# Weight gradients of a backward pass moved into the staging slots of the K and V gradients

## Chip, core and metric

The kernel runs on one core of a Trainium2 chip. The metric is the device time of one execution in microseconds, as the median of several runs; besides, one execution is recorded by the hardware profiler, and all views below are of that execution.

## The reference, cut to what matters

Two layers, each an attention over a long cache followed by a small dense block, are applied twice to one token with the same weights; the kernel computes the output and the gradients of the loss for the input, both caches and all weights.

```python
x = x + attention(layernorm(x), k_cache, v_cache, wq, wo)   # L1
x = x + mlp(layernorm(x), w1, b1, w2, b2)                   # L2: h = relu(n w1 + b1)^2; h w2 + b2
x = x + attention(layernorm(x), k_cache, v_cache, wq, wo)   # L3, same weights
x = x + mlp(layernorm(x), w1, b1, w2, b2)                   # L4, same weights
out, vjp = jax.vjp(f, x, k_cache, v_cache, wq, wo, w1, b1, w2, b2)
return out, *vjp(grad_out)
```

Sizes: D = 1024, 32 query heads in G = 4 groups of R = 8, head width 128, 65536 cached positions, F = 3584, all in bfloat16. Each cache has 67 MB, and so has its gradient. There is one token, so every weight gradient is an outer product, and as each weight is used in two layers, it is the sum of two outer products: a contraction over two rows. The four weight gradients together have 31.5 MB: `out_4` for wq (1024 x 4096), `out_5` for wo (4096 x 1024), `out_6` for w1 (1024 x 3584), `out_8` for w2 (3584 x 1024).

## The kernel before

The caches are streamed four times: forward for L1, forward for L3, a backward pass for L3 (`attn_bwd3`) and a last pass (`attn_bwd4`) that reads K and V once more and makes the gradients of both caches for both layers. The change is in this last pass and in what leads up to it.

SBUF is cut into 14 areas of 1 MB (128 partitions x 4096 bf16 elements). Two neighbours make a pair of 2 MB, so `pair[6]` is `area[6]` and `area[7]`. The exponentials of the two forward passes lie in `e_tiles`, one 1 MB tile a group and layer, and become free group by group in the last pass. A `Ring` hands out areas for reads in the order of their last use; `ring.once` adds areas that are used for one read and then leave it. A `Turn` hands out its areas in a circle. A read is issued by SP as soon as its area is free, in the order of the program; so the number of free areas sets how far reads run ahead.

The last pass goes over 256 items, 64 to a group, of 8 blocks of 128 positions. `pipeline` interleaves three steps: `vT` transposes the item's V, `vS` two items later makes the products with the output gradient and, every fourth item, the coefficients X (VectorE and, for the copies at L1033 and L1034, GpSimd) and their transposes, and `k8`, 7 items after `vT`, makes the query gradient and the cache gradients: matmuls at L1071 into `ps_gg`, evacuated by `evac` (L152 on ScalarE, L155 on VectorE, whichever has less planned load) into a staging slot. `ST` is a turn of three slots, `pair[6]`, `pair[8]` and `pair[10]`. Every four items fill one slot with 1 MB of K's and 1 MB of V's gradient, which GpSimd's queue (POOL) writes by two DMAs (L1078, L1079). Further tasks are hung on item numbers by `at(bg, i, fn)` and are put behind what is then queued on each engine (`in_order`).

The weight gradients are such tasks. `rows_into` first brings two vectors that lie across the partitions into two rows: it takes four columns at a time, with two casts (L1092), four matmuls with the identity (L1095) and one evacuation of 2 x 512. `outer2` then makes units of 128 x 1024, two matmuls (L1122) and an evacuation each, and writes every stage of 128 x 2048 (512 KB) by a DMA of POOL (L1126). The stages are five half-areas: four in the tiles `e_tiles` of the first group, free when that group is done, and one in `area[5]`. So the tasks run from item 73 on and are spread evenly up to item 244; the last group's part of wq follows the last item.

```python
ring.once(area[6], area[8], area[9], area[10], area[11])
for st, b in ((1, 0), (1, 1), (0, 0), (1, 2), (0, 1)):
    streams[st].fetch(ORD4[0], b)
...
at(bg, done[0], rows_ready)
i0, i1 = done[0] + 1, IPG * G - 12
tasks = list(gw_tasks())
for t, fn in enumerate(tasks):
    at(bg, i0 + t * (i1 - i0) // len(tasks), fn)
```

Before the first item, the first five halves of K and V are read ahead into the once-areas, and the ring's five areas are filled further; `og1.first` and `g_setup` prepare the first group. The rows of wo for the second group (`og1.later`) come as 256 KB DMAs into `first_rows` on SP's queue, up to 30 items ahead; the other rows of wo and wq go through `wo_rows`, three areas of 256 KB, on ScalarE's queue.

Of the kernel before, what the change touches and what calls it, by code (L numbers as in the profile page):

```python
# [8 lines left out]
BF = mybir.dt.bfloat16  # L9
# [5 lines left out]
P = 128  # L15
# [3 lines left out]
def kernel(  # L19
# [39 lines left out]
    GD = R * DH  # L59
# [8 lines left out]
    IPG = C // 8  # L68
    TLEAD = 2
    LAGV = TLEAD + IPG + 12  # L70
    SLOT = 4096
    OG = 2048
    SMALL = 8192

    def spool(name, bufs=1):
# [4 lines left out]
    tmp = spool("tmp", bufs=2)  # L80
# [8 lines left out]
    def ps_tr():  # L89
        return PS["pool"].tile([P, 8, P], BF, name="ps_tr", tag="tr", bufs=2 if PS["pass4"] else 3)  # L90
# [4 lines left out]
    def ps_gg():  # L95
        return PS["pool"].tile([P, 1024], F32, name="ps_gg", tag="gg", bufs=2)
# [26 lines left out]
    ident_b = const.tile([P, P], BF, name="ident_b")  # L123
# [18 lines left out]
    def evac(out, in_, kind="bf"):  # L142
        n = 1
        for d in in_.shape[1:]:
            n *= d
        if kind == "bf":
            ca, cd = 0.19 + n * 0.00081, 0.15 + n * 0.00053
        else:
            ca, cd = 0.19 + n * 0.00081, 0.15 + n * 0.00105
        if load["act"] + ca <= load["dve"] + cd:  # L150
            load["act"] += ca
            nc.scalar.copy(out=out, in_=in_)  # L152
# [10 lines left out]

    main = spool("main")
    ECP = R * CP
    e3_all = main.tile([P, G * ECP], BF, name="eT3")
    e_tiles = {1: [main.tile([P, ECP], BF, name="eT1_%d" % g)[:, :] for g in range(G)],
               3: [e3_all[:, g * ECP:(g + 1) * ECP] for g in range(G)]}
    area, pair, wides = [], {}, []
    for i in range(0, 14, 2):  # L170
        t = main.tile([P, 2 * SLOT], BF, name="pair%d" % i)
# [11 lines left out]
    def part(ap, i, n):  # L183
        return ap[:, i * n:(i + 1) * n]
# [70 lines left out]
    ring = Ring()  # L255
# [331 lines left out]
    def at(bg, i, fn):  # L587
        bg.setdefault(i, []).append(fn)
# [371 lines left out]
    def attn_bwd4(La, Lb, oga, ogb, order, eTa, eTb, dqT, bg, group_done, streams):  # L960
        lname = "B1"
        kit = items_of(order)
        n = len(kit)
# [5 lines left out]
        ST = Turn([pair[6], pair[8], pair[10]])  # L969
        DOB = vec.tile([P, G, 4, R2], BF, name="DOB")  # L970
        nc.vector.memset(DOB[:], 0.0)
        state = {}
# [127 lines left out]
    def outer2(stages, out_dram, a_rows, K, b_rows, c0, N):  # L1100

        KB = K // P
        ov = out_dram.rearrange("(p k) n -> p k n", k=KB)
        av = a_rows[:, 0:K].rearrange("q (p k) -> q k p", k=KB)
        st = {}
        pieces = []
        if 2 * N <= OG:
            per = OG // N
            pieces = [(kb, per, 0, N) for kb in range(0, KB, per)]
        else:  # L1110
            pieces = [(kb, 1, n0, min(OG, N - n0)) for kb in range(KB) for n0 in range(0, N, OG)]
        for kb, per, n0, w in pieces:
            for kk in range(per):
                for m0 in range(0, w, 1024):
                    def unit(kb=kb, per=per, n0=n0, w=w, kk=kk, m0=m0):
                        if kk == 0 and m0 == 0:
                            st["og"] = stages.next()
                        nn = min(1024, w - m0)
                        pg = ps_gg()
                        for q0 in range(0, nn, 512):  # L1120
                            qq = min(512, nn - q0)
                            nc.tensor.matmul(pg[:, q0:q0 + qq], lhsT=av[:, kb + kk, :],  # L1122
                                             rhs=b_rows[:, n0 + m0 + q0:n0 + m0 + q0 + qq], start=True, stop=True)
                        evac(st["og"][:, kk * w + m0:kk * w + m0 + nn], pg[:, 0:nn], kind="f32")
                        if kk == per - 1 and m0 + 1024 >= w:
                            nc.gpsimd.dma_start(out=ov[:, kb:kb + per, c0 + n0:c0 + n0 + w],  # L1126
                                                in_=st["og"][:, 0:per * w].rearrange("p (k n) -> p k n", n=w))
                    yield unit


    open_psum("psA")
# [3 lines left out]
    eT1, eT3 = Exps(1), Exps(3)  # L1135
# [5 lines left out]
    L1 = new_layer(x0, "L1")  # L1141
    ORD1, ORD2, ORD3, ORD4 = [0, 1, 2, 3], [3, 2, 1, 0], [0, 1, 2, 3], [3, 2, 1, 0]
# [88 lines left out]
    bg = {}  # L1231
# [67 lines left out]
    ring.add(area[7], area[12])  # L1299
# [3 lines left out]
    ring.once(area[6], area[8], area[9], area[10], area[11])  # L1303
# [9 lines left out]
    og1 = OutGrad(L1, "B1")  # L1313
    vbx1 = part(area[13], 3, 1024)
    og1.first(ORD4[0], dx1, vbx1)
    ring.remove(area[7], area[12])
# [3 lines left out]
    col_to_dram(gb1, F, out_7, nc.gpsimd)  # L1320

    PS["pool"].release()
    open_psum("ps4", pass4=True)
    load["act"] = load["dve"] = 0.0

    long_rows, short_rows = area[12], part(area[13], 0, 1024)
    wo_rows = Turn([part(area[13], i, 1024) for i in (1, 2)] + [part(area[5], 1, 1024)])
    e_first = [e_tiles[k][ORD4[0]] for k in (1, 3)]
    stages = Turn([part(e, i, OG) for i in range(2) for e in e_first] + [area[5][:, SLOT - OG:SLOT]])
    dqT1 = vec.tile([P, HQ], F32, name="B1_dqT")  # L1330

    def rows_ready():
        nc.gpsimd.memset(long_rows, 0.0)
        nc.gpsimd.memset(short_rows, 0.0)

    def gwq_tasks(gs, fresh=True):
        gs = sorted(gs)
        a, b = gs[0] * R, (gs[-1] + 1) * R
        if fresh:
            yield from rows_into(short_rows, [L3["n"][:], L1["n"][:]], DC)  # L1340
        yield from rows_into(long_rows, [dqT3[:, a:b], dqT1[:, a:b]], b - a)
        yield from outer2(stages, out_4, short_rows, D, long_rows, gs[0] * GD, len(gs) * GD)

    def gw_tasks():
        yield from rows_into(short_rows, [gx[:], dx2[:]], DC)
        yield from rows_into(long_rows, [L4["g"][:], L2["g"][:]], FC)
        yield from outer2(stages, out_8, long_rows, F, short_rows, 0, D)
        yield from rows_into(short_rows, [L4["n"][:], L2["n"][:]], DC)
        yield from rows_into(long_rows, [dh4[:], dh2[:]], FC)
        yield from outer2(stages, out_6, short_rows, D, long_rows, 0, F)  # L1350
        yield from gwq_tasks(ORD4[0:2])
        yield from rows_into(short_rows, [dx3[:], dx1[:]], DC)
        yield from rows_into(long_rows, [L3["oT"][:], L1["oT"][:]], HQ)
        yield from outer2(stages, out_5, long_rows, QD, short_rows, 0, D)
        yield from gwq_tasks(ORD4[2:3])

    bg = {}
    LAG4 = 7
    first_rows = Turn(wo_rows.areas + [part(area[12], i, 1024) for i in range(4)])
# [5 lines left out]
    at(bg, done[0], rows_ready)  # L1365
    i0, i1 = done[0] + 1, IPG * G - 12
    tasks = list(gw_tasks())
    for t, fn in enumerate(tasks):
        at(bg, i0 + t * (i1 - i0) // len(tasks), fn)
# [18 lines left out]

    attn_bwd4(L1, L3, og1, og3, ORD4, eT1, eT3, dqT1, bg, group_done, streams)

    for t in gwq_tasks(ORD4[-1:], False):
        t()
    for p in (main, tmp, vec, const, PS["pool"]):
        p.release()

# [29 lines left out]
```

## Time and profile before

| | |
|---|---|
| median of three runs | 2000.78 us (1998.74 to 2001.92) |
| profiled execution | 2006.47 us, span 2004.7 us |
| busy PE, PEld | 1599.8 us (80%), 1320.6 us (66%) |
| busy DVE, ACT, POOL | 1108.3 us (55%), 1032.3 us (51%), 203.3 us (10%) |
| DMA | 798.08 MB, mean 398 GB/s; 628.11 MB read, 165.69 MB written |
| chain that ended last | PE 39%, DMA 30%, DVE 12%, ACT 11%, issue 7% |

PE is TensorE's matmuls and PEld its weight loads, DVE is VectorE, ACT ScalarE, POOL GpSimd, SP SyncE. Times in views are microseconds from the start of the span. The last pass begins at about 1225. A view by windows gives, for each stretch, its length, the busy time and the number of instructions of the five engines, the clock granted to TensorE as a share of full speed, the mean busy share of the 16 DMA engines (rounding takes it a little over 1) and what they moved. In a timeline the second number is a duration, and the brackets hold the idle time before an instruction and what ended it.

### The profile page before, as it was taken

Reading aid. Unit: us, or ns where it says so; the run is one execution under the profiler, and the core shown is the slowest. Engines: PE = TensorE matmul, PEld = TensorE weight load, DVE = VectorE, ACT = ScalarE, POOL = GpSimd, SP = SyncE. Lnnn points to the kernel's source line nnn. Section 1 sums busy time; section 2 is a strip of 40 time slices with the busy share of each in tenths; the row PEclk is TensorE's granted clock in tenths of the full one; section 3 lists DMA queues with packets and bytes.
Section 4 is the critical chain, followed back from the end, with each engine's and each line's share of the span. In section 5 each row is a group of like instructions: output and inputs, shape, how many; then the busy total and the mean of one; then the engine's idle time right before and its main releaser. Section 6 shows DMA issues by size and latency. Waiting matters only on the chain.

```text
span 2004.7 us, 66048 instructions
## 1 busy us (share of the span) xinstructions
PE 1599.8 (80%) x30052; PEld 1320.6 (66%) x30052; DVE 1108.3 (55%) x1826; ACT 1032.3 (51%) x1290; POOL 203.3 (10%) x362
## 2 busy tenths in 40 slices
PE   7888776678888867887878876877888878778896
PEld 6888776578787756876777774555555545545463
DVE  4544431255444313745454446876677767787675
ACT  3543432125433313445454436876677667767775
POOL 0000000000000000000000001222122222212221
PEclk9999997679999976998989987999889988899898
DMA  9999999999999996999999996999999999999997
GB/s 395 426 424 421 419 422 413 395 368 376 424 421 419 423 414 272 399 418 409 411 413 393 403 372 261 389 425 424 389 413 407 423 423 383 422 358 422 423 422 293
DMA packets 117316, 798.08 MB, mean 398 GB/s; under 512 B 11548, under 2 KB 11562, under 8 KB 55082
## 3 DMA queue, kind: packets, MB, share of 16 engines
q1 hardware_dynamic: 80986, 608.22, 74.0%
q0 software_dynamic: 29136, 173.04, 20.9%
q10 hardware_dynamic: 6912, 12.59, 1.7%
q8 instruction: 235, 3.85, 0.7%
q14 instruction: 47, 0.39, 0.0%
HBM read 628.11 MB, written 165.69 MB: 396 GB/s over the span
## 4 chain that ended last, share of the span: by engine, by line
PE 39%; DMA 30%; DVE 12%; ACT 11%; issue 7%; POOL 0%; SPq 0%; DVEq 0%; ACTq 0%; POOLq 0%
DMA pair<-in_A_v_cache_dram 13%; DMA out_dram<-pair 8%; PE ps_tr L656 7%; DMA pair<-in_A_k_cache_dram 5%; PE ps_sc L675 4%; ACT small L152 4%; PE ps_tr L909 4%; PE ps_acc L718 3%; PE ps_gg L1071 3%; PE ps_tr L1004 3%; ACT pair L152 3%; DVE pair L155 3%; DVE small L155 2%; PE ps_sc L930 2%; PE ps_gg L1122 2%
## 5 line engine op out<-in xcount | busy, mean ns | idle before, releaser
L155 DVE COPY small<-ps_tr 128x1024 bf16<-128x1024 bf16 x655 | 445.2, 688 | 356.1 <-PE ps_tr L656 197.8
L152 ACT COPY small<-ps_tr 128x1024 bf16<-128x1024 bf16 x385 | 386.6, 1014 | 410.1 <-PE ps_tr L656 234.1
L152 ACT CAST pair<-ps_gg 128x1024 bf16<-128x1024 f32 (+2 forms) x331 | 320.2, 983 | 143.2 <-PE ps_gg L1071 81.8
L155 DVE CAST pair<-ps_gg 128x1024 bf16<-128x1024 f32 x245 | 289.2, 1181 | 115.6 <-PE ps_gg L1071 89.0
L656 PE MATMUL ps_tr<-ident_b,pair 128*128 128x128 bf16 x3456 | 263.4, 225 | 34.6 <-DMA pair<-in_A_k_cache_dram 25.4
L1071 PE MATMUL ps_gg<-pair,small 64*128 64x512 bf16 x1024 | 202.9, 405 | 53.8 <-ACT pair L152 21.5
L656 PEld LDWEIGHTS <-pair 128*128 128x128 bf16 x3456 | 209.5, 101 | 39.7 <-DMA pair<-in_A_k_cache_dram 27.8
L675 PE MATMUL ps_sc<-L_qpad,small 128*128 128x64 bf16 (+7 forms) x3712 | 187.5, 194 | 27.1 <-ACT small L152 13.9
L718 PE MATMUL ps_acc<-eT,pair 128*128 128x64 bf16 x3840 | 167.1, 205 | 44.9 <-DMA pair<-in_A_v_cache_dram 39.6
L718 PEld LDWEIGHTS <-pair 128*128 128x128 bf16 x3840 | 151.9, 104 | 48.5 <-DMA pair<-in_A_v_cache_dram 42.4
L675 PEld LDWEIGHTS <-small 128*128 128x128 bf16 x3712 | 151.5, 99 | 38.5 <-ACT small L152 20.1
L1004 PE MATMUL ps_tr<-ident_b,pair 128*128 128x128 bf16 x1792 | 163.3, 229 | 14.1 <-DMA pair<-in_A_v_cache_dram 12.0
L422 ACT ACTIVATE pair<-pair 128x1024 bf16<-128x1024 bf16 (+1 forms) x125 | 142.1, 1137 | 45.6 <-DVE pair L421 43.6
L909 PE MATMUL ps_tr<-ident_b,pair 128*128 128x128 bf16 x2048 | 153.5, 227 | 10.4 <-DMA pair<-in_A_v_cache_dram 5.4
L1004 PEld LDWEIGHTS <-pair 128*128 128x128 bf16 x1792 | 115.6, 102 | 60.5 <-issue 41.5
L909 PEld LDWEIGHTS <-pair 128*128 128x128 bf16 x2048 | 126.7, 102 | 30.8 <-issue 20.7
L1071 PEld LDWEIGHTS <-small 64*128 64x128 bf16 x1024 | 60.5, 94 | 111.3 <-issue 83.8
L930 PE MATMUL ps_sc<-B_dOpad,small 128*128 128x64 bf16 (+7 forms) x2048 | 103.0, 194 | 21.5 <-DVE small L155 13.9
L1024 PE MATMUL ps_sc<-DOB,small 128*128 128x64 bf16 (+3 forms) x2048 | 111.7, 194 | 0.1
L1024 PEld LDWEIGHTS <-small 128*128 128x128 bf16 x2048 | 86.6, 99 | 36.8 <-issue 32.2
L930 PEld LDWEIGHTS <-small 128*128 128x128 bf16 x2048 | 81.2, 99 | 32.8 <-DVE small L155 17.5
L681 DVE TENSOR_REDUCE pm_all<-pair 128x8 f32<-128x512 f32 x64 | 44.0, 688 | 106.1 <-ACT pair L680 106.1
(262 smaller groups left out, 1966.2 us busy)
## 6 DMA issues: line engine op xcount, KB each, us to landing
pair<-in_A_v_cache_dram SPq DMA_DIRECT2D x70, 2048.0 KB, 19.9
pair<-in_A_k_cache_dram SPq DMA_DIRECT2D x65, 2048.0 KB, 19.5
out_dram<-pair POOLq DMA_DIRECT2D x128, 1024.0 KB, 16.2
pair<-in_A_k_cache_dram SPq DMA_DIRECT2D x97, 1024.0 KB, 12.4
pair<-in_A_v_cache_dram SPq DMA_DIRECT2D x96, 1024.0 KB, 12.8
pair<-in_A_wo_dram SPq DMA_DIRECT2D x24, 1024.0 KB, 20.3
out_dram<-eT POOLq DMA_DIRECT2D x44, 512.0 KB, 15.6
pair<-in_B_w_dram SPq DMA_DIRECT2D x24, 896.0 KB, 16.7
```

Source lines behind the costliest of these rows:

```text
L152: nc.scalar.copy(out=out, in_=in_)
L155: nc.vector.tensor_copy(out=out, in_=in_)
L422: nc.scalar.activation(out=view, in_=view, func=ACTF.Copy, accum_out=ycol)
L656: nc.tensor.transpose(pt[:, i, :], kb8[:, i, :], ident_b[:, :])
L675: nc.tensor.matmul(ps_s[:, slot:slot + w, :].rearrange("p a b -> p (a b)"), lhsT=kt[:, i, :], rhs=L["qpad"][:, g, 0:w, :].rearrange("p a b ...
L681: nc.vector.tensor_reduce(out=pm_all[:, :, c0 // UB], in_=S_sb[:, :, c0:c0 + un], axis=AX.X, op=ALU.max)
L718: nc.tensor.matmul(ps_o[:, :, :].rearrange("p a b -> p (a b)"), lhsT=vb8[:, i, :], rhs=eT[g][:, :, c:c + 8], start=(c == 0), stop=(c == C ...
L909: nc.tensor.transpose(pt[:, i, :], vb8[:, i, :], ident_b[:, :])
L930: nc.tensor.matmul(ps_dp[:, slot:slot + w, :].rearrange("p a b -> p (a b)"), lhsT=vt[:, i, :], rhs=dOpad[:, g, 0:w, :].rearrange("p a b -> ...
L1004: nc.tensor.transpose(pt[:, i, :], vb8[:, i, :], ident_b[:, :])
L1024: nc.tensor.matmul(ps_dp[:, slot:slot + w, :].rearrange("p a b -> p (a b)"), lhsT=vt[:, i, :], rhs=DOB[:, g, 0:w, :].rearrange("p a b -> p ...
L1071: nc.tensor.matmul(pg[:, t2 * 512:(t2 + 1) * 512], lhsT=xt[64 * t2:64 * t2 + 64, blk0 + half, :], rhs=GG[64 * t2:64 * t2 + 64, :, :, :].re ...
```

## The change

The weight gradients are staged in the slots of K's and V's gradients, 2 MB at a time, and begin at item 3.

- `outer2` returns a list of slots, each a list of units, takes its slot from `ST`, and has the contraction run over 64 partitions, 0 to 63 or 64 to 127 (`at_row`). A slot holds 8 rows of 1024 columns, 2 of 3584, 4 of 2048 or 8 of 1024, and is written by one DMA. 15 slots are hung on fixed items, four units to an item; two slots of 1 MB follow the last item.
- `rows_moved` replaces `rows_into`, but for the last group: all columns of both vectors are copied into one tile (2 copies), transposed at once, copied out, and two small DMAs on POOL move them into two rows, on partitions 0 and 1 or 64 and 65 of `long_rows` and `short_rows`. So the next product's rows can be put in place while the other pair is in use. `rows_a` and `rows_b` run ahead of the pass.
- After the first group, `ST` has a fourth slot, `e_pair`, in the tiles of that group's exponentials.
- `pair[6]` must be free from item 3 on, so `area[6]` leaves `ring.once`, and four halves are read ahead instead of five. `area[12]` becomes `long_rows` earlier; `area[13]` takes its place in the ring before the pass.
- `wo_rows` has five areas, and the second group's rows of wo come through it on ScalarE's queue, 8 items ahead.

```diff
-    for st, b in ((1, 0), (1, 1), (0, 0), (1, 2), (0, 1)):
+    for st, b in ((1, 0), (1, 1), (0, 0), (1, 2)):
...
+    def rows_moved(rows, cols, nj, queue=None):
+        cc = tmp.tile([P, 64], BF, name="rm_cc")
+        for l in range(2):
+            nc.vector.tensor_copy(out=cc[:, l * nj:(l + 1) * nj], in_=cols[l])
+        pt = ps_tr()
+        nc.tensor.transpose(pt[0:2 * nj, 0, :], cc[:, 0:2 * nj], ident_b[:, :])
+        flat = tmp.tile([64, P], BF, name="rm_flat")
+        nc.vector.tensor_copy(out=flat[0:2 * nj, :], in_=pt[0:2 * nj, 0, :])
+        for l in range(2):
+            (queue or nc.gpsimd).dma_start(out=rows[l:l + 1, 0:nj * P], in_=flat[l * nj:(l + 1) * nj, :])
...
+        def unit(kb, n, kk, m0):
+            if kk == 0 and m0 == 0:
+                st["og"] = ST.next()
...
+                nc.tensor.matmul(pg[:, q0:q0 + qq], lhsT=av[:, kb + kk, :],
+                                 rhs=b_rows[rows, m0 + q0:m0 + q0 + qq], start=True, stop=True, tile_position=(at_row, 0))
...
+    rows_a()
+    rows_b()
...
-    og1.later(vbx1, ORD4[1], bg, 16, 5, first_rows, 30, nc.sync)
+    og1.later(vbx1, ORD4[1], bg, 14, 5, wo_rows, 8, nc.scalar)
...
+    slots_a = outer2(out_8, long_rows, F, short_rows, 0, D, 64, 8)
+    slots_b = outer2(out_6, short_rows, D, long_rows, 0, F, 0, 2)
+    slots_c = outer2(out_5, long_rows, QD, short_rows, 0, D, 64, 8)
+    early = slots_a + slots_b + slots_c + outer_q(ORD4[0:2], 4) + outer_q(ORD4[2:3], 8)
+    when = [3, 11, 19, 31, 47, 59, 75, 87, 99, 115, 131, 147, 163, 179, 219]
+    for i, slot in zip(when, early):
+        for k, fn in enumerate(slot):
+            at(bg, i + k // 4, fn)
+    at(bg, 35, rows_c)
+    at(bg, 90, rows_d)
+    at(bg, done[1] + 1, lambda: rows_q(ORD4[0:2]))
+    at(bg, done[2] + 1, lambda: rows_q(ORD4[2:3]))
...
     def group_done(j):
-        if j == 1:
+        if j == 0:
+            ST.areas.append(e_pair)
+        elif j == 1:
```

More of the change, by code (lines that the diff above doesn't have):

```diff
@@ L71 @@
     SLOT = 4096
-    OG = 2048
     SMALL = 8192
@@ L165 @@
     ECP = R * CP
-    e3_all = main.tile([P, G * ECP], BF, name="eT3")
-    e_tiles = {1: [main.tile([P, ECP], BF, name="eT1_%d" % g)[:, :] for g in range(G)],
+    e3_all = main.tile([P, (G + 1) * ECP], BF, name="eT3")
+    e_tiles = {1: [main.tile([P, ECP], BF, name="eT1_%d" % g)[:, :] for g in range(G - 1)] + [e3_all[:, G * ECP:]],
                3: [e3_all[:, g * ECP:(g + 1) * ECP] for g in range(G)]}
+    e_pair = e3_all[:, (G - 1) * ECP:(G - 1) * ECP + 2 * SLOT]
     area, pair, wides = [], {}, []
@@ L968, in attn_bwd4 @@
         NDT = Turn([part(small, i, 512)[0:64, :].rearrange("p (s r) -> p s r", r=R2) for i in (14, 15)])
-        ST = Turn([pair[6], pair[8], pair[10]])
         DOB = vec.tile([P, G, 4, R2], BF, name="DOB")
@@ L1098, in rows_into, with outer2 @@
             yield lambda j0=j0: piece(j0)
-    def outer2(stages, out_dram, a_rows, K, b_rows, c0, N):
+    def outer2(out_dram, a_rows, K, b_rows, c0, N, at_row, per):
         KB = K // P
         ov = out_dram.rearrange("(p k) n -> p k n", k=KB)
-        av = a_rows[:, 0:K].rearrange("q (p k) -> q k p", k=KB)
+        rows = slice(at_row, at_row + 64)
+        av = a_rows[rows, 0:K].rearrange("q (p k) -> q k p", k=KB)
         st = {}
[L1106 to L1128, printed above, removed]
@@ new lines, in unit @@
+        def unit(kb, n, kk, m0):
+            if kk == 0 and m0 == 0:
+                st["og"] = ST.next()
+            nn = min(1024, N - m0)
+            pg = ps_gg()
+            for q0 in range(0, nn, 512):
+                qq = min(512, nn - q0)
+                nc.tensor.matmul(pg[:, q0:q0 + qq], lhsT=av[:, kb + kk, :],
+                                 rhs=b_rows[rows, m0 + q0:m0 + q0 + qq], start=True, stop=True, tile_position=(at_row, 0))
+            evac(st["og"][:, kk * N + m0:kk * N + m0 + nn], pg[:, 0:nn], kind="f32")
+            if kk == n - 1 and m0 + 1024 >= N:
+                nc.gpsimd.dma_start(out=ov[:, kb:kb + n, c0:c0 + N],
+                                    in_=st["og"][:, 0:n * N].rearrange("p (k n) -> p k n", n=N))
@@ L1131 @@
+        slots = []
+        for kb in range(0, KB, per):
+            n = min(per, KB - kb)
+            slots.append([lambda kb=kb, n=n, kk=kk, m0=m0: unit(kb, n, kk, m0) for kk in range(n) for m0 in range(0, N, 1024)])
+        return slots
     open_psum("psA")
@@ L1298 @@
     dh2 = dhidden(pg2[:, :], L2, "B2")
-    ring.add(area[7], area[12])
+    long_rows, short_rows = area[12], part(area[13], 0, 1024)
+    nc.gpsimd.memset(long_rows, 0.0)
+    ring.add(area[7], area[13])
     w1 = slabs(B_w1, 0, DC, 0, F)
@@ L1302 @@
     streams = (Stream(Kv), Stream(Vv))
-    ring.once(area[6], area[8], area[9], area[10], area[11])
-    for st, b in ((1, 0), (1, 1), (0, 0), (1, 2), (0, 1)):
+    ring.once(area[8], area[9], area[10], area[11])
+    for st, b in ((1, 0), (1, 1), (0, 0), (1, 2)):
         streams[st].fetch(ORD4[0], b)
@@ L1315 @@
     og1.first(ORD4[0], dx1, vbx1)
-    ring.remove(area[7], area[12])
+    ring.remove(area[7], area[13])
     gb2 = add_cols(gx[:], dx2[:], "gb2")
@@ L1320, with rows_a, rows_b, rows_c @@
     col_to_dram(gb1, F, out_7, nc.gpsimd)
+    nc.gpsimd.memset(short_rows, 0.0)
+    def rows_a():
+        rows_moved(short_rows[64:66, :], [gx[:], dx2[:]], DC)
+        rows_moved(long_rows[64:66, :], [L4["g"][:], L2["g"][:]], FC)
+    def rows_b():
+        rows_moved(short_rows[0:2, :], [L4["n"][:], L2["n"][:]], DC)
+        rows_moved(long_rows[0:2, :], [dh4[:], dh2[:]], FC)
+    def rows_c():
+        rows_moved(short_rows[64:66, :], [dx3[:], dx1[:]], DC)
+        rows_moved(long_rows[64:66, :], [L3["oT"][:], L1["oT"][:]], HQ)
+    def rows_d():
+        rows_moved(short_rows[0:2, :], [L3["n"][:], L1["n"][:]], DC)
+    def rows_q(gs):
+        sl = slice(min(gs) * R, (max(gs) + 1) * R)
+        rows_moved(long_rows[0:2, :], [dqT3[:, sl], dqT1[:, sl]], len(gs) * R)
+    def outer_q(gs, per):
+        return outer2(out_4, short_rows, D, long_rows, min(gs) * GD, len(gs) * GD, 0, per)
+    rows_a()
+    rows_b()
     PS["pool"].release()
@@ L1324 @@
     load["act"] = load["dve"] = 0.0
[L1326 to L1329, printed above, removed]
+    wo_rows = Turn([part(area[13], i, 1024) for i in (1, 2)] + [part(area[5], i, 1024) for i in (1, 2, 3)])
+    ST = Turn([pair[6], pair[8], pair[10]])
     dqT1 = vec.tile([P, HQ], F32, name="B1_dqT")
[L1332 to L1355, printed above, removed]
     bg = {}
     LAG4 = 7
-    first_rows = Turn(wo_rows.areas + [part(area[12], i, 1024) for i in range(4)])
-    og1.later(vbx1, ORD4[1], bg, 16, 5, first_rows, 30, nc.sync)
+    og1.later(vbx1, ORD4[1], bg, 14, 5, wo_rows, 8, nc.scalar)
     og1.later(vbx1, ORD4[2], bg, IPG + 14, 4, wo_rows, 8, nc.scalar)
@@ L1364 @@
     done = [IPG * (j + 1) + LAG4 + 1 for j in range(G)]
[L1365 to L1369, printed above, removed]
+    slots_a = outer2(out_8, long_rows, F, short_rows, 0, D, 64, 8)
[3 more added lines that the diff above has]
+    when = [3, 11, 19, 31, 47, 59, 75, 87, 99, 115, 131, 147, 163, 179, 219]
+    assert len(early) == len(when) and len(slots_a) == len(slots_b) == len(slots_c) == 4
+    for i, slot in zip(when, early):
[5 more added lines that the diff above has]
+    at(bg, done[2] + 1, lambda: rows_q(ORD4[2:3]))
     qg1.early(ORD4[0:1], bg, done[1] + 16, 2.75, vbx1, wo_rows, 5)
@@ L1389 @@
     attn_bwd4(L1, L3, og1, og3, ORD4, eT1, eT3, dqT1, bg, group_done, streams)
-    for t in gwq_tasks(ORD4[-1:], False):
-        t()
+    g = ORD4[-1]
+    for t in rows_into(long_rows, [dqT3[:, g * R:(g + 1) * R], dqT1[:, g * R:(g + 1) * R]], R):
+        t()
+    for slot in outer_q([g], 4):
+        for t in slot:
+            t()
     for p in (main, tmp, vec, const, PS["pool"]):
```

## The prediction

> **What bounds the kernel now.** I read the page's slices first: the last pass is the right-hand 40% of this row.
>
> ```profile
> DMA  9999999999999996999999996999999999999997
> GB/s 395 426 424 421 419 422 413 395 368 376 424 421 419 423 414 272 399 418 409 411 413 393 403 372 261 389 425 424 389 413 407 423 423 383 422 358 422 423 422 293
> ```
>
> The DMA engines are full nearly everywhere; the exceptions in the pass are slice 25 (261 GB/s), slice 36 (358) and the last (293). So I cut the end of the kernel into five stretches by windows: before the pass, its start, group 0, the rest, the tail.
>
> ```profile
> 1190.00:1230.00 40.00, 20.92 (x299) 17.99 (x300) 30.30 (x74) 26.36 (x34) 3.36 (x6) 0.71 1.01 402
> 1230.00:1260.00 30.00, 25.78 (x423) 18.86 (x421) 21.86 (x30) 20.91 (x23) 5.29 (x10) 0.98 0.35 130
> 1260.00:1420.00 160.00, 129.99 (x2001) 89.52 (x2002) 120.58 (x179) 116.07 (x131) 41.02 (x66) 0.98 1.01 421
> 1420.00:1966.00 546.00, 452.22 (x5595) 288.31 (x5592) 398.43 (x571) 385.90 (x448) 129.37 (x228) 0.91 1.00 407
> 1966.00:2004.70 38.70, 25.58 (x282) 13.93 (x279) 21.28 (x35) 18.61 (x20) 7.24 (x12) 0.76 0.64 255
> ```
>
> Columns: stretch, length, busy us of PE, PEld, DVE, ACT, POOL, clock, DMA share, GB/s. From 1260 to 1966 the share is 1.00 to 1.01: the pass goes at the speed of the transfers, and engine time saved there buys nothing. What can be won or lost is idle DMA: 0.65 x 30 = 19.5 us at the start, 0.36 x 38.7 = 13.9 us in the tail, a few us between. The start, closer:
>
> ```profile
> 1225.00:1230.00 5.00, 3.12 (x25) 2.50 (x26) 3.47 (x18) 1.75 (x3) 1.34 (x3) 0.50 0.99 381
> 1230.00:1235.00 5.00, 3.43 (x62) 3.24 (x60) 3.32 (x7) 1.08 (x2) 0.00 (x0) 0.86 0.06 23
> 1235.00:1240.00 5.00, 4.71 (x81) 3.55 (x81) 2.13 (x4) 3.55 (x4) 0.00 (x0) 1.00 0.01 3
> 1240.00:1245.00 5.00, 4.31 (x67) 2.84 (x65) 3.54 (x6) 4.17 (x5) 1.21 (x2) 1.00 0.01 3
> 1245.00:1250.00 5.00, 4.92 (x86) 3.51 (x84) 4.78 (x6) 4.05 (x5) 1.10 (x2) 1.00 0.46 184
> ```
>
> Everything that can be read ahead has landed by 1230, and nothing can be written until item 10 has filled the first slot. POOL's timeline and SP's give the two ends of the hole, the first write and the first read that a freed slot lets go:
>
> ```profile
> 1246.71 0.55 POOL L1078 DMA_DIRECT2D out_dram<-pair  x1 [3.22 <-ACT pair L152]
> ...
> 1254.03 0.33 SPq L272 DMA_DIRECT2D pair<-in_A_k_cache_dram  x1
> ```
>
> **The change, part by part.** The bytes of the pass stay as they are, so the sum is of idle DMA time gained and lost, at 424 GB/s (the page's best slices): 1 MB is 2.5 us, a 2 MB slot 5 us.
>
> *Read-ahead lost.* area[6] is no longer lent to the once-slots: four K/V halves of 1 MB are read ahead instead of five, 2.5 us. And og1.later's first rows, which SP issued from 1215.5 on, are now fetched on ACT's queue from item 6 on:
>
> ```profile
> pair<-in_A_wo_dram SPq DMA_DIRECT2D x7, 256.0 KB, 7.5
> ```
>
> 1.84 MB, 4.3 us. The engines are what the 1190 to 1230 stretch waits for (DVE is busy 30.3 of 40 us, and the chain goes through its rows there), so less to read does not shorten it: 6.8 us of transfers move from before 1230 into the full stretch. Bounds 2.5 (rows that arrive when the queue has a gap anyway) and 6.8; I take 6.8, since the queue is at 1.01 afterwards. Its ACT issues (0.33 us each, 8 of them) lie in ACT's idle time.
>
> *Rows by transposes.* rows_a and rows_b add ahead of the pass 8 copies into columns, 4 transposes, 4 copies out and 8 small DMAs on POOL. The copies are like L1092's casts, 0.16 us, some 2 us of DVE. The wait is worse: rm_flat has two buffers, so in DVE's new order the third copy waits until the first two small DMAs have landed, and the V evacuations of the pass are queued behind it, with PE's products and POOL's copies behind those. These DMAs stand on POOL behind its first two copies (1224.0 to 1225.2), at 0.52 us an issue; the nearest row, L333's 2 KB write, lands after 4.9 to 5.6 us in a full queue. So DVE goes on at about 1231 to 1232 where it evacuates the first V item at 1228.2. Bounds 0 (landing at once) and 4 us; I take 2.5, for DVE is idle 1.7 us of the next 5 and catches up some.
>
> *First weight slot, items 3 and 4.* 8 units: each two matmuls (x2 in 0.59 us in the tail at full clock, 1.01 at half clock), and a cast of 1.02 us on ACT or 1.22 on DVE: 9.0 us of casts, about 4 on ACT and 5 on DVE. Between 1230 and 1245 ACT is idle 6.2 us, DVE 6.0, PE 2.6. So PE is short: 8 x 0.59 = 4.7 against 2.6 idle gives 2.1 us at least; at half clock (0.50 at 1225 to 1230, and PE waits for DVE here) 8.1 against 2.6 gives 5.5. I take 3.5 us by which the first K/V write comes later. In return 2 MB, 5 us, are written in the hole.
>
> *Second slot, items 11 and 12.* Another 8 units ahead of the release of the ring slot at item 15: engines at 1245 to 1260 are busy 12 to 13 of 15 us, so 2 to 4 us more until reads go on, against up to 4.9 us of idle DMA left there that its 2 MB can fill. I put the two against each other, 0.
>
> Start: 6.8 + 2.5 + 3.5 - 5 = 7.8 us later. Bounds: 2.5 + 0 + 2.1 - 5 - 3 = -3.4, and 6.8 + 4 + 5.5 - 5 + 4 = 15.3.
>
> *Group 0.* Six weight slots now go through the three staging slots that K and V share until e_pair joins. For K, K, W the engines need 8.4 + 8.4 us (POOL's copies at L1033 come every 8.2 to 9.2 us for 4 items) plus some 4.5; DMA needs 10 MB, 24.7 us. A slot may thus be in flight 24.7 - 8 = 16.7 us, and the waits say that slots already hold the engines up:
>
> ```profile
> ACT pair L152 <- DMA out_dram<-pair: 23.7, 13, 4.2
> ```
>
> As long as two full slots are in flight behind a wait, the queue stays full. Bounds 0 and 6 x 4 = 24 us; I take 2.
>
> *Removed.* 40 row pieces by L1095 and L1092 (40 casts of 0.6 us, 80 of 0.16) and 5 half-size stages, all where DMA is at 1.00: 1 us for the dips after 1427 (share 0.83 to 0.92 for 10 us, with row pieces in it). The 3.53 us memset of the long rows at 1389.7 lies in the full stretch: 0. Writes of 14 to 16 KB a partition instead of 3 to 4: the rate is 421 without weight writes and 407 with them, but the windows from 1550 to 1600 have 423 to 424 with weight writes in them, so most of it is not theirs: 3 us of a bound of 18.
>
> The Trainium skill's page "DMA: Bandwidth & Descriptors" (Anatomy of one DMA) gives every POOL-side DMA a fixed 2 us beside its bytes; with 62 weight DMAs made into 17 that would be an estimate of 45 x 2 = 90 us less if none overlapped. The trace disagrees, as 422 GB/s at a share of 1.02 between 1850 and 1875 with 512 KB writes in it leaves no gap to take away.
>
> *Tail.* The last weight rows go out as two DMAs of 1 MB instead of four of 512 KB, and the last 35 items carry no weight work: 1 us (0 to 4), since the tail waits for its casts and the last landing either way.
>
> Sum: 7.8 + 2 - 1 - 3 + 1 = 6.8 us. The profiled execution takes 2006.47 us (span 2004.7 and 1.8 around it), 5.7 above the median of the runs; the same 6.8 on 2000.78 gives 2007.6, and 2013.3 for a profiled one.
>
> **Rivals.** (1) *The hole swallows the weight work* (faster). If DVE's wait is under 1 us and the casts of both slots fit into the 12 us in which ACT and DVE idle, the start gains: 10 us written in the hole, against 6.8 of read-ahead and 2.1 of PE. With 1 us of smaller dips and 3 of longer runs: 5 us less, 1996, with group 0 and the tail at nothing. For it: engines idle in 1230 to 1245; against: PE busy 12.5 of 15 us. It decides if the first K/V write is issued before about 1249.
> (2) *Longer runs lift the rate* (faster). If the 407 GB/s after 1420 comes from the 4 KB writes, 546 x (1 - 407/421) = 18 us come back; less 8 at the start: 10 us less, 1991. For it: the step at 1420; against: the windows at 424 with these writes.
> (3) *Three slots are too few* (slower). If each weight slot in group 0 makes the engines wait so long that the queue runs empty and PE falls to half clock, as after 1420 (clock 0.50 to 0.64 for 7.5 us), 3 us for each of six: 18 on top of 6.8, less some overlap: 2020. For it: 16 us landings against 16.7 allowed.
> (4) *Bytes only move* (no change). Losses and gains cancel, within 0.2%, which is 4 us and about what a measurement tells from no change: 2001.
>
> **How the numbers follow.** The forecast (2003 to 2016) 0.52, (3) 0.10, (4) 0.15, (1) 0.13, (2) 0.10. Slower by over 0.2%: the forecast's and (3)'s, 0.60, as the part of the forecast's range under 4 us is counted with (4), 0.17; faster: 0.23. The range takes in (1) and most of (3), and leaves out (2) and the far end of (3): 1995 to 2019.
>
> **What would show it.** Right: DMA share in the 30 us from the end of reading ahead below 0.35 or the hole over 25 us long in idle DMA, the first K/V write at 1250 to 1254, weight DMAs from about 1242, a DVE wait on small DMAs before the first evacuation, share 1.0 from 1270 to 1940. Wrong: a first K/V write before 1249, or over 415 GB/s from 1420 on (rival 2), or DMA share under 0.95 in group 0 (rival 3).

## The result and the profile after

| | before | after |
|---|---|---|
| median of four runs each | 2001.35 us (1998.74 to 2003.09) | 2050.49 us (2046.6 to 2056.58) |
| ratio to before | | 1.0247, 95% interval 1.023 to 1.0264 |
| profiled execution | 2006.47 us, span 2004.7 | 2056.58 us, span 2054.8 |
| granted clock, mean | 0.908 | 0.88 |

The change makes the kernel 2.5% slower, some 49 us; I had forecast 7 us. The page's slices after the change:

```profile
DMA  9999999989999997999999975889899999999996
GB/s 397 424 424 421 417 426 411 390 337 425 420 424 421 416 418 273 404 407 411 412 412 388 410 284 209 329 353 370 318 399 393 424 424 423 400 423 420 423 379 279
```

A slice is now 51.4 us. Where the row of before was back at 425 two slices after the start of the pass (slice 27), there are now seven slices (25 to 31) between 209 and 399 GB/s, and only then 424. Cut into stretches as before (length, busy us of PE, PEld, DVE, ACT, POOL, clock, DMA share, GB/s):

```profile
1190.00:1228.00 38.00, 21.13 (x281) 18.68 (x280) 28.36 (x73) 25.72 (x33) 5.62 (x10) 0.59 0.84 322
1228.00:1260.00 32.00, 29.15 (x300) 19.02 (x300) 19.82 (x28) 16.58 (x17) 5.07 (x9) 0.68 0.24 88
1260.00:1420.00 160.00, 124.51 (x1410) 76.10 (x1410) 96.03 (x130) 93.97 (x105) 30.04 (x54) 0.80 0.87 345
1420.00:2016.00 596.00, 494.32 (x6220) 312.18 (x6220) 421.99 (x545) 414.56 (x466) 121.03 (x212) 0.89 0.99 402
```

The stretch from 1260 to 1420 ran at a share of 1.01, 421 GB/s and clock 0.98. It is now at 0.87, 345 and 0.80, with fewer instructions done on every engine (PE 1410 for 2001). So neither the engines nor the transfers set the pace there; both wait for something. The start:

```profile
1225.00:1230.00 5.00, 1.21 (x13) 1.05 (x11) 1.25 (x5) 1.01 (x1) 1.49 (x3) 0.50 0.48 182
1230.00:1235.00 5.00, 5.00 (x38) 3.08 (x36) 2.38 (x7) 1.01 (x1) 1.73 (x4) 0.50 0.01 3
1235.00:1240.00 5.00, 5.00 (x38) 3.22 (x38) 2.73 (x4) 2.31 (x3) 0.00 (x0) 0.50 0.00 0
1240.00:1245.00 5.00, 5.00 (x32) 2.47 (x31) 2.66 (x4) 2.65 (x3) 0.00 (x0) 0.50 0.01 3
```

From 1230 PE is busy all the time and at half clock until 1245, where the clock was 0.86 to 1.00 before. The first writes of POOL and the first read of SP that a freed slot lets go:

```profile
1246.30 0.56 POOL L1130 DMA_DIRECT2D out_dram<-pair  x1 [14.57 <-issue]
1257.01 0.55 POOL L1077 DMA_DIRECT2D out_dram<-pair  x1 [3.26 <-ACT pair L151]
...
1261.57 0.33 SPq L272 DMA_DIRECT2D pair<-in_A_v_cache_dram  x1
```

The first weight slot goes out at 1246.30, but the first K and V only at 1257.01, after 1246.71 before. The waits of ScalarE and VectorE for staging slots (total, times, longest):

```profile
ACT pair L151 <- DMA out_dram<-pair: 54.8, 11, 8.7
...
DVE pair L154 <- DMA out_dram<-pair: 50.8, 11, 9.8
```

Before, ScalarE's were 23.7 us with a longest of 4.2, and VectorE's 14.3 with a longest of 2.4.

**Where the time is.** POOL's timeline gives the issue of every K write (64 in the pass, 16 a group; where a slot is written in two halves, the second is counted). Counted from the copy of the first group's row products that opens the pass (1225.8 before, 1223.3 after), in us:

| kernel | to the first K write | 1st to 16th | 16th to 32nd | 32nd to 48th | 48th to 64th | to the end |
|---|---|---|---|---|---|---|
| before | 20.9 | 142.0 | 197.1 | 222.7 | 179.9 | 16.3 |
| after | 33.7 | 216.9 | 191.4 | 198.2 | 171.5 | 19.8 |
| late slots (first experiment) | 25.6 | 146.0 | 239.1 | 238.7 | 163.1 | 19.2 |
| own 2 MB slot (fifth) | 25.1 | 145.8 | 216.1 | 234.7 | 166.9 | 24.1 |
| 1 MB slots, halves apart (seventh) | 31.6 | 178.6 | 201.0 | 201.2 | 166.2 | 16.3 |
| own 0.5 MB pieces, rows in the pass (twelfth) | 21.1 | 147.8 | 200.3 | 213.0 | 186.6 | 15.7 |
| half the weights' matmuls (fifteenth) | 35.7 | 208.4 | 193.4 | 200.3 | 171.2 | 17.7 |

After against before: 12.8 us at the start and 74.9 in group 0 are lost, 5.7 + 24.5 + 8.4 in the later groups come back, the tail loses 3.5, and the pass opens 2.6 earlier: 50, as the spans say. Five weight slots are written within those 16 writes of group 0, 8.9 MB.

**Bytes and idle DMA.** Between the first and the 16th K write the trace moves 58.0 MB before and 73.2 MB after: the weight writes, and reads that came elsewhere before. The 15.2 MB more are 36 us at 424 GB/s, so 39 of the 74.9 us are more than bytes. About 29 of them are idle DMA (a mean share of 0.86 over 216.9 us, for 0.99 over 142.0); the rest is a lower rate while the DMA engines are busy. Behind group 0 the trace has 230.8 MB for 245.5, 14.7 MB less, which is 35 us: all that the later groups and the tail give back. From 1190 to the end the share is 0.96 of 814.7 us before and 0.91 of 864.8 us after, so about 33 and 78 us are idle. These 45 us are nearly all of the loss.

**One turn of the three slots.** POOL's writes, two of a K and V slot counted once:

```profile
1270.12 0.53 POOL L1130 DMA_DIRECT2D out_dram<-pair  x1 [7.31 <-ACT pair L151]
1274.74 0.53 POOL L1077 DMA_DIRECT2D out_dram<-pair  x1 [4.09 <-ACT pair L151]
...
1282.66 0.53 POOL L1077 DMA_DIRECT2D out_dram<-pair  x1 [6.86 <-ACT pair L151]
...
1308.88 0.53 POOL L1130 DMA_DIRECT2D out_dram<-pair  x1 [22.81 <-DVE pair L154]
```

All three slots are handed over within 12.5 us, and then nothing for 26. In between both evicting engines stand still, and PE behind them (timeline of all engines):

```profile
1290.55 1.01 ACT L151 CAST pair<-ps_gg 128x1024 bf16<-128x1024 f32 x1 [6.41 <-DMA out_dram<-pair]
1290.59 1.23 DVE L154 CAST pair<-ps_gg 128x1024 bf16<-128x1024 f32 x1 [4.86 <-DMA out_dram<-pair]
1291.61 1.01 PE L1126 MATMUL ps_gg<-pair 64*128 64x512 bf16 x2 [4.97 <-ACT pair L151]
```

and by windows of 2.5 us:

```profile
1287.50:1290.00 2.50, 0.00 (x0) 0.00 (x0) 0.00 (x0) 0.00 (x0) 0.00 (x0) 0.85 1.00 423
...
1297.50:1300.00 2.50, 2.50 (x18) 1.45 (x17) 1.97 (x2) 1.17 (x2) 0.00 (x0) 0.50 0.22 92
1300.00:1302.50 2.50, 2.50 (x17) 1.27 (x15) 0.69 (x1) 1.44 (x2) 0.00 (x0) 0.50 0.00 0
1302.50:1305.00 2.50, 2.50 (x13) 0.87 (x11) 1.56 (x2) 0.33 (x1) 0.00 (x0) 0.50 0.22 43
```

From 1287.5 every engine waits for a landing while the DMA engines work off what is queued; from 1290.5 the engines fill two slots at once, the weights' and K's and V's, neither of which can be written before it is full, and no ring area is given back (SP issues no read from 1284.7 to 1303.6). At 1298 the queue is empty, 11 us before the next write is issued. The same happens, more mildly, from 1322 to 1340. Two sides that should overlap take turns.

### The profile page after: what moved, and what is told of

Same layout as the page of the kernel before. It is cut to its first block, busy times and chain, and to the rows that moved or that the text cites. A ratio compares the mean times of both kernels' runs of the same rounds, so it can differ in the third digit from the quotient of the medians.

```text
span 2054.8 us, 65624 instructions
## 1 busy us (share of the span) xinstructions
PE 1635.9 (80%) x29909; PEld 1323.7 (64%) x29909; DVE 1102.7 (54%) x1756; ACT 1031.3 (50%) x1273; POOL 186.8 (9%) x335
## 5 line engine op out<-in xcount | busy, mean ns | idle before, releaser
L154 DVE COPY small<-ps_tr 128x1024 bf16<-128x1024 bf16 x639 | 434.3, 688 | 356.3 <-PE ps_tr L656 193.5
L151 ACT COPY small<-ps_tr 128x1024 bf16<-128x1024 bf16 x401 | 402.6, 1013 | 435.5 <-PE ps_tr L656 233.4
L151 ACT CAST pair<-ps_gg 128x1024 bf16<-128x1024 f32 x297 | 297.2, 1014 | 180.3 <-PE ps_gg L1070 96.0
L154 DVE CAST pair<-ps_gg 128x1024 bf16<-128x1024 f32 (+1 forms) x225 | 271.5, 1210 | 159.3 <-PE ps_gg L1070 69.0
L1070 PE MATMUL ps_gg<-pair,small 64*128 64x512 bf16 x1024 | 210.7, 421 | 87.2 <-DVE pair L154 39.0
L1023 PE MATMUL ps_sc<-DOB,small 128*128 128x64 bf16 (+3 forms) x2048 | 121.3, 201 | 0.1
L1126 PE MATMUL ps_gg<-pair 64*128 64x512 bf16 x240 | 90.2, 473 | 14.0 <-ACT pair L151 9.0
```

The costliest lines, as they stand in the source:

```text
L1023: nc.tensor.matmul(ps_dp[:, slot:slot + w, :].rearrange("p a b -> p (a b)"), lhsT=vt[:, i, :], rhs=DOB[:, g, 0:w, :].rearrange("p a b -> p ...
L1070: nc.tensor.matmul(pg[:, t2 * 512:(t2 + 1) * 512], lhsT=xt[64 * t2:64 * t2 + 64, blk0 + half, :], rhs=GG[64 * t2:64 * t2 + 64, :, :, :].re ...
```

## The experiments

Theories, as the expectations name them: **S**, weights share the turn of 2 MB slots with K and V and so make engines wait for landings; **B**, bursts of four units an item hold up K and V; **P**, rows and read-ahead at the start of the pass; **Q**, GpSimd's queue holds X copies and K and V writes behind weight DMAs; **C**, TensorE at half clock is what makes it long; **G** and **W** are on K's and V's own slots. Ratios are to the kernel before, run on the same chip, with 95% intervals.

**1. All weight slots from item 75 on.**

```diff
-    when = [3, 11, 19, 31, 47, 59, 75, 87, 99, 115, 131, 147, 163, 179, 219]
+    when = [75, 83, 91, 99, 107, 115, 123, 131, 141, 157, 173, 187, 149, 165, 219]
-    at(bg, 35, rows_c)
-    at(bg, 90, rows_d)
+    at(bg, 104, rows_c)
+    at(bg, 135, rows_d)
```

> All 15 weight slots start at item 75 or later, when the fourth slot is there; rows ahead of the pass and four halves read ahead stay as in the changed kernel. Theory S (three slots shared with K and V in group 0 make the engines wait for landings, and the queue runs empty behind that): group 0 falls from 217 us back to about 142 to 150 and the time to 1995-2010, since the 26 us of bytes go back to the later groups. Theory B (four units put into one item, and X copies of GpSimd behind the weight DMA, cost about 4 us a slot wherever the slot stands): the cost moves with the slots, 2030-2055. Theory P (rows ahead of the pass and the lost read-ahead are most of it): the first K write stays at +30 us or later, and the time at 2030 or more.

Measured: 2055.22 us, ratio 1.0267 (1.0241 to 1.0293), at the end of B's range. Group 0 is back at 146.0, as S said, but the time isn't: the next two groups take 239 us each, although there are four slots then. Windows of this run:

```profile
1250.00:1420.00 170.00, 137.91 (x1998) 91.20 (x1999) 122.51 (x164) 120.64 (x133) 38.16 (x67) 0.95 1.01 419
1420.00:1600.00 180.00, 153.46 (x1572) 89.38 (x1570) 114.29 (x147) 111.40 (x122) 32.23 (x58) 0.78 0.92 360
```

The full stretch and the dry one have changed places. So placing weight work early is not what costs, nor the number three alone: 2 MB slots in a common turn cost where they stand.

**2. The same, rows of the first two gradients within the pass.**

```diff
-    rows_a()
-    rows_b()
+    at(bg, 66, rows_a)
+    at(bg, 69, rows_b)
```

> As the one before, but the rows of the first two weight gradients are made at items 66 and 69 and not ahead of the pass. Theory P prices the rows at 4 us or more below the run before; theory S at the 3.5 us by which the first V eviction came later, at most.

Measured: 2058.78 us, 1.0284 (1.025 to 1.0318). The first K write comes at 21.1, as before the change, so rows ahead of the pass cost 4.5 us there. But the time is the same as the first run's within the intervals, not 4 us shorter as P had it: group 0, at whose end the rows now stand, takes 167.4 us for 146.0, and the next group 222.5 for 239.1. A line of VectorE's timeline shows rows made close together beside 2 MB writes:

```profile
1401.81 0.21 DVE L1093 COPY rm_flat<-ps_tr 16x128 bf16<-16x128 bf16 x1 [10.21 <-DMA pair<-rm_flat]
```

Rows of 2 to 8 KB stand behind megabytes, and VectorE with all its evictions stands behind them.

**3. Six slots of 1 MB in place of three of 2 MB.**

```diff
-    ST = Turn([pair[6], pair[8], pair[10]])
+    ST = Turn(area[6:12])
# K and V written every two items, 0.5 MB each; outer2's slots cut in two, units at the same items
```

> The changed kernel with each 2 MB slot cut into two of 1 MB (six, later eight), K and V written in halves of 0.5 MB, weights in 1 MB; every unit stays at the item where it was. Theory S: what is held while a slot is filled is halved, so more of the six is landing or free: group 0 gains 20 to 45 us of its 217, the time 2005-2030. Theory B (bursts, order of GpSimd's queue): units and their order stay, so 2040-2055.

Measured: 2030.47 us, 1.0144 (1.012 to 1.0169). 20 us come back with every unit where it was; 35 of the 75 us lost in group 0 (181.7 us there). That is S's end at 2030 and under B's range.

**4. One unit an item, 2 MB slots.** `at(bg, i + k // 4, fn)` becomes `at(bg, i + k, fn)`; rows_c at 41, rows_d at 97.

> The changed kernel with one unit an item in place of four, so a weight slot is open for eight items in place of two. Theory S: each slot is held about 13 us longer while it is filled, so slower, 2055-2085. Theory B: the bursts are gone, 2015-2035.

Measured: 2072.96 us, 1.0366 (1.0329 to 1.0404). Slower, as S said: a weight slot is open for eight items, so for longer two slots are being filled and at most one is in flight.

**5. As 1, but the weights have the fourth slot to themselves.**

```diff
+    SW = Turn([e_pair])
-                st["og"] = ST.next()
+                st["og"] = SW.next()
-        if j == 0:
-            ST.areas.append(e_pair)
```

> As the first experiment (all weight slots at item 75 or later, four units an item), but the weights have the fourth 2 MB slot for themselves, and K and V keep the three others for themselves, as before the change. The first experiment showed that a weight slot costs about 5 us wherever it stands, so theory S is now: sharing one turn makes an eviction for K, V or weights wait for the landing of the other's 2 MB. If so, the own slot takes that away: group 1 and 2 of the pass go from 239 and 239 us to about 200 and 222, the time to 2005-2020. Theory B (a burst of eight units holds up K and V, so no reads are freed and PE falls to half clock, whoever owns the slot): 2040-2055.

Measured: 2040.74 us, 1.0209 (1.0181 to 1.0237). Against the first run 12 to 14 us come back (by ratios and by medians): that is what the shared turn is worth. Most of the loss stays, as B said.

**6. As 5, two units an item and slots 11 items apart.** `at(bg, i + k // 2, fn)`, `when` from 75 to 228 in steps of 8 to 13, the later rows moved along.

> As the run before this, with two units an item in place of four and the slots 11 items apart in place of 8 to 16. Theory S: as the run before or up to 5 us better, 2000-2020. Theory B: half the burst, so about half the loss, 2020-2035 where the run before is 2040-2055.

Measured: 2030.66 us, 1.0154 (1.012 to 1.0188). That is in B's range and outside S's, but the edit changes the spacing of the slots along with the burst.

**7. As 3, the second half of each slot four items after the first.** `at(bg, i + 4 * (k // 4), fn)`; rows_c at 40, rows_d at 96.

> As the third experiment (1 MB slots, 2030 us), but the second half of each weight slot is made four items after the first and not in the next item, so weights come in bursts of 1 MB. Theory B: the burst is halved, 2010-2022. Theory S: the number of slots in use is the same over ten items, 2022-2032.

Measured: 2018.32 us, 1.0093 (1.0068 to 1.0118): 10 to 12 us for making 1 MB at a time, as B had it.

**8. As 3, the weights' writes on ScalarE's queue.** `nc.scalar.dma_start` for the DMA of `unit`.

> As the third experiment (1 MB slots, 2030 us), but the weights' writes are issued on ScalarE's queue, so GpSimd's X copies and K and V writes no longer stand behind them. In the third experiment's trace transposes of X waited up to 11.5 us for an X copy of GpSimd. Theory Q (GpSimd's order): 10 us or more better, 2005-2020. Theories S and B: 2025-2035.

Measured: 2032.58 us, 1.0169 (1.0137 to 1.0201). Q falls: with 1 MB slots, the weights' writes on GpSimd's queue are not a cost by themselves.

**9. As 3, one unit an item.** rows_c at 41, rows_d at 97.

> The third experiment (1 MB slots, 2030 us) with one unit an item in place of four; every slot begins at the item where it began, and is open for four items, as one of K and V is for two. Theory B (bursts hold up K and V): 2005-2015, below the 2018 us of the run with the halves four items apart. Theory S (slots held): the fourth experiment lost 22 us by the same edit with 2 MB slots, so 2030 or more.

Measured: 2020.88 us, 1.0098 (1.0075 to 1.0121). With 1 MB slots the edit gains 10 us against the third run, with 2 MB slots it lost 22: a spread of units pays only if the slot is small. It is no better than 7, and lies between the ranges of B and S.

**10. As 9, slots spread over items 16 to 230,** the rows moved along.

```diff
+    when = [16, 31, 47, 62, 77, 93, 108, 124, 139, 155, 170, 186, 201, 214, 230]
```

> As the run before this, with the 15 slots spread evenly over the pass, items 16 to 237, so nothing of them in the first 35 us. Theory B: the first K write comes at about +25 us as without early weights (the rows stay ahead of the pass) in place of +32, and the sum is 2000-2010. If the early start were a gain by itself, it would be slower than the run before this.

Measured: 2025.96 us, 1.0109 (1.0084 to 1.0134). The first K write came at 25.6, as expected, but that was given back later: the same as 9 within the intervals, not 2000 to 2010. 8.7 us of it are one wait of TensorE, ending at 1927.5, for rows made six items before their use; the next run shows the same fault.

**11. As 5, the slot cut into four of 0.5 MB, one unit every 1.37 items.**

```diff
+    SW = Turn([part(e_pair, i, 2048) for i in range(4)])
+            at(bg, i + int(1.37 * k), fn)
```

> As the fifth experiment (weights in a fourth slot of their own, from item 75 on, 2041 us), with that slot cut into four of 0.5 MB and one unit every 1.37 items: bursts and sizes as in the kernel before, rows, read-ahead and row loads as in the changed one. Theory B: the rest of the loss of the own slot goes, but for the 4 to 5 us of the rows ahead of the pass and some 4 us of read-ahead: 2002-2012. If it stays over 2020, something else of the change costs (rows within the pass, the loads on ScalarE's queue).

Measured: 2020.63 us, 1.0088 (1.0073 to 1.0103), above what B gave. One place stands out, in TensorE's timeline:

```profile
1922.59 1.04 PE L1132 MATMUL ps_gg<-pair 64*128 64x512 bf16 x2 [12.13 <-DMA pair<-rm_flat]
```

I had made the rows for the third group's wq two items before their use. The small DMA landed behind the writes, TensorE waited, and the DMA engines fell to a share of 0.15 to 0.20 from 1918 to 1928.

**12. As 11, rows in better places.** rows_a and rows_b at items 55 and 65, the third group's rows at 203 for a first use at 231 (wo's gradient goes after the first part of wq's).

> As the eleventh experiment (weights in four pieces of 0.5 MB of their own, from item 75 on, 2021 us), with two edits to the rows: the first two pairs are made within the pass, ten items apart, and not ahead of it; and the rows of the third group's query are made some 28 items before their first use, not two (in the eleventh run TensorE waited 12.2 us on that small DMA, and the DMA engines ran empty behind it). If the account is right, the first K write comes at +21 us in place of +25 and the stall of about 13 us goes: 2001-2006, the kernel before within what can be measured. If something of the change that I haven't named costs, 2010 or more.

Measured: 2006.3 us, 1.0032 (1.0018 to 1.0047). The account closes but for 6.4 us. The table puts 5.8 in group 0, which holds no weight slot here; the differences of the later groups nearly cancel. What differs there from before is the shorter read-ahead and the first rows; runs 1 and 11, with no rows in this group, lose 4.0 and 3.8 there. By exclusion that is left for the read-ahead; no run gives the fifth half back.

**13. As 5, all eight units in one item.** `at(bg, i, fn)`.

> The fifth experiment (2 MB weight slot of its own, four units an item, 2041 us) with all eight units of a slot in one item. Theory B (the burst holds up K and V until the reads and writes already queued run out): 8 to 20 us slower, 2049-2061. If the burst does not matter and only the 2 MB that a slot holds do: 2036-2045.

Measured: 2042.23 us, 1.0204 (1.0182 to 1.0226), as run 5, so B's 2049 to 2061 is missed. Past four units an item a larger burst costs nothing more.

**14. The kernel before with K and V in six slots of 1 MB.**

> The kernel before with K and V staged in six slots of 1 MB in place of three of 2 MB; the weights' 0.5 MB stages as they were. Theory G (the 2 MB unit of K and V is itself too coarse: engines wait for landings 24 us in ACT's rows of before): faster, 1985-1997. Theory W (K and V alone run at the DMA engines' rate in the first group, 425 GB/s, so smaller writes with 4 KB runs only add packets): same or slower, 1998-2012.

Measured: 2010.06 us, 1.005 (1.0032 to 1.0067). W holds: without weights in the turn smaller slots cost 9 us. So the third and seventh run gain in spite of that.

**15 and 16. Half of the weights' matmuls left out,** in the changed kernel and in the one before:

```diff
-            for q0 in range(0, nn, 512):
+            for q0 in range(0, 512, 512):
-            evac(st["og"][:, kk * N + m0:kk * N + m0 + nn], pg[:, 0:nn], kind="f32")
+            evac(st["og"][...].rearrange("p (a n) -> p a n", n=512),
+                 pg[:, 0:512].unsqueeze(1).to_broadcast([P, nn // 512, 512]), kind="f32")
```

> The changed kernel with half of the weights' matmuls left out: each unit makes its first 512 columns and the eviction copies them twice, so evictions, slots, order and bytes are the same. In the dry stretches of the changed kernel TensorE is busy 2.5 of 2.5 us at clock 0.50, and a weight matmul then takes about 0.5 us, so that 116 units leave out some 60 us of it. Theory C (TensorE at half clock is what holds up K and V after each wait for a landing): 2010-2030. Theory S (only the landings and the size of the slots hold up): 2042-2052.

> The kernel before with the same half of the weights' matmuls left out. The DMA engines are at a share of 0.98 to 1.00 there from 1250 on, so both theories expect little: 1994-2001.

Measured: 2051.27 us, 1.0245 (1.0228 to 1.0262), and 2000.32, 0.9992 (0.9982 to 1.0001). C falls for the weights' share: nothing is gained. The windows of run 15 still have the same holes, with TensorE at half clock on what is left to it:

```profile
1297.50:1300.00 2.50, 2.50 (x19) 1.52 (x17) 1.26 (x2) 1.98 (x3) 0.00 (x0) 0.50 0.29 118
1300.00:1302.50 2.50, 2.50 (x26) 1.98 (x24) 1.58 (x2) 0.87 (x1) 0.00 (x0) 0.50 0.00 0
```

**17. As 12, in bursts again** (`i + int(1.37 * (k - k % 8)) + k % 8 // 4`), **and 18. as 12, two pieces of 1 MB** (`SW = Turn([part(e_pair, i, SLOT) for i in range(2)])`).

> The twelfth experiment (weights in four 0.5 MB pieces of their own, evenly spread, 2006 us) with the units in bursts again: eight in two items, then none for nine items. Theory B (the burst): 2020-2032, near the run with a 2 MB slot and two units an item. Theory S (how much is staged in one piece): 2004-2010.

> The twelfth experiment with two pieces of 1 MB in place of four of 0.5 MB, units evenly spread as there. Theory S: half the way to a slot of 2 MB, 2012-2025. Theory B: 2004-2010.

Measured: 2011.51 us, 1.0069 (1.0043 to 1.0094), and 2011.68 us, 1.0069 (1.005 to 1.0088). Each alone costs 5 us by the medians and 7 by the ratios (17's interval still touches that of 12), so run 17 lies between the ranges of S (to 2010) and B (from 2020), and run 18 between those of B (to 2010) and S (from 2012). Neither explains the 34 us between runs 5 and 12. The table gives 4 of these to the rows at the start and 8 to the end, where in run 5 the last weight slots share one area and ScalarE waits 6.5 us for its landing. The rest isn't separated: run 5 has one area of 2 MB for the weights and run 12 four of 0.5 MB, so the size of a piece, the number of areas and the bursts change together. Waiting for the weights' own areas is not the difference, at 18.1 us in all in run 5 and 27.7 in run 18. Another part may be VectorE's waits for rows of wo and wq, which no run tests by themselves: 14.3 us in run 5 (24.0 in run 1), none in runs 12 and 18, 11.3 before and 6.4 in the changed kernel.

**The DMA engines in these runs,** by windows from 1190 to the end of each:

| run | weight slots | share | GB/s |
|---|---|---|---|
| before | five of 0.5 MB | 0.96 | 392 |
| after | 2 MB, shared | 0.91 | 368 |
| 1, 4 | 2 MB, shared, late or one unit an item | 0.92, 0.91 | 368, 363 |
| 3, 7, 9 (K and V in 1 MB too) | 1 MB, shared | 0.96, 0.96, 0.96 | 383, 385, 384 |
| 5, 6, 13 | one own of 2 MB, four, two or eight units an item | 0.93, 0.93, 0.93 | 377, 376, 375 |
| 12, 17 | four own of 0.5 MB, spread or in bursts | 0.95, 0.96 | 390, 391 |
| 18 | two own of 1 MB, spread | 0.96 | 390 |
| 14 (before, K and V in 1 MB) | five of 0.5 MB | 0.98 | 387 |

Share and rate tell two kinds of loss apart. With 2 MB weight slots, shared or own, the share is 0.91 to 0.93, whatever the burst (run 6 is profiled in its slowest execution): the loss is mostly idle DMA. Run 3 leaves every unit where it was, halves the slots, and the share is back at 0.96. What runs 3, 7 and 9 still lose is then a lower rate at the same share, and run 14 has this too, without weights in the turn; so it comes with K's and V's smaller writes. What lowers the rate is not shown.

## Why the prediction was wrong

The step that failed is *Group 0*. I took 2 us with 24 as the far end; 74.9 were lost there, and 39 of them are more than bytes. Its argument was that a slot "may thus be in flight 24.7 - 8 = 16.7 us" and that the queue stays full "as long as two full slots are in flight behind a wait". That counts slots as if they were filled one after the other. But a weight slot is filled while K's and V's is half full; with two of three open, only one can be in flight. In the turn shown above its 2 MB and the reads queued with it lasted 7.5 us (to 1298), against the 18 in which the two were filled (1290.5 to 1308.9). That one turn has 6.4 us of idle DMA from 1297.5 to 1305 (0.78 + 1.00 + 0.78 of 2.5 us).

Runs 3, 4 and 9 bear this out from both sides: halved slots gave back 20 us and most of the idle DMA, and a slot that stays open for longer lost 22 us with 2 MB but gained 10 with 1 MB. Run 5 shows that the shared turn is not the whole of it: with three slots for K and V alone, an own 2 MB slot of the weights still leaves the share at 0.93. In one stretch of that run nothing is written from 1623.6 to 1645.5 while the weights' slot and K's and V's are both being filled (VectorE stands for 4.9 us of it waiting for a row of wo), and the DMA share falls as low as 0.38. How the cost divides between the slot's size and its being the only area stays open.

Rival 3 named the mechanism and its sign (a share under 0.95 in group 0; it was 0.87), with 3 us for each slot, where the 29 us of idle DMA are some 6 for each of the five slots. That the change is slower was forecast, but from the start of the pass, which lost 10.3 us to the first K write (1257.01 for 1246.71); most of the 49 us lie elsewhere, so the right sign is in good part luck.

Point by point:
- *Read-ahead lost*, 6.8: about 4, by exclusion. It doesn't show at the start (first K write at 21.1 in run 2, 20.9 before) but in group 0 (146.0 and 145.8 in runs 1 and 11 for 142.0).
- *Rows by transposes*, 2.5 with 4 as far end: 4.0 to 4.5 (runs 1 against 2, 11 against 12). The waits I expected are there: the first V eviction of VectorE came at 1229.14, not 1228.2, on a pass that opened 2.6 us earlier.
- *First weight slot*, 3.5 later with 5.5 as far end: 8.1 (33.7 against 25.6 without early slots). PE stayed at half clock until 1245, the worse of my two cases and longer than it.
- *Second slot*, 0: not measured apart. It is the slot written at 1270.12, with which the turn shown above begins.
- *Removed and longer runs*, 4 gained together: nothing shows. The later groups and the tail gave back 35.1 us, and the 14.7 MB less that they moved are 35 us.
- *Tail*, added to the sum as 1 lost, with 4 as far end: 3.5 lost.
- Rival 1 falls with a first K write at 1257, rival 2 with 402 GB/s after 1420.

The Trainium skill's page "DMA: Bandwidth & Descriptors" (Bandwidth) has the rule to batch DMAs to 1 MiB or more, from measurements of reads into SBUF. For K's and V's writes run 14 goes that way: 0.5 MB in place of 1 MB cost 9 us. For the weights' writes it doesn't: run 18 has 1 MB in place of run 12's 0.5 MB and is 5 us slower, and 62 weight DMAs made into 17 went with 49 us more. The Trainium skill's page "TensorE: Matmul & The Clock Gate" (HAM oscillation) tells of a kernel in which waits for transfers return the clock to half each time. The trace agrees: in the 4.97 us without a matmul before 1291.61 the clock falls, and it is 0.50 from 1290 to 1307. Run 15 takes half of the weights' matmuls off TensorE and gains nothing, so their share of the half clock is not what costs.

What stays open: how much the half clock on K's and V's own matmuls lengthens a turn, since nothing here kept the clock up through a wait; how size, number of areas and bursts share the loss of an own 2 MB slot; and what lowers the rate of K's and V's 0.5 MB writes. No version beat the kernel before; run 12 comes within 0.3%.

## What to carry to other kernels

A staging slot is not free when it is merely not in flight: count, at each wait, how many slots are open and how many bytes are queued, and compare these bytes with the time until the next slot can be handed over. A second producer in the same turn adds an open slot, so give it its own small pieces; here that gave back all but 6 us. Larger weight writes saved nothing here, where the queue was already full. And a tiny DMA on the queue of large writes can land as late as they do (up to 22.6 us here), so what it feeds should be made that far ahead.

## Not expected

- With 1 MB slots GpSimd itself waits for earlier writes to land before it issues the second of a pair, which with 2 MB slots came to 6.7 us in all (before). The waits of run 3:

```profile
POOL out_dram L1079 <- DMA out_dram<-pair: 81.6, 41, 4.1
```

- The small row DMAs, 8 to 32 rows of 256 bytes, took 1.7 us to land with an empty queue and up to 22.6 us beside the writes (changed kernel).
- Leaving out half of the weights' matmuls, 116 matmuls of 512 columns, moved the time of neither kernel by more than 0.1%, though PE is busy for 80% of the span in both.
